# Attention and rational MoE on one core: the plan names each tile's buffer, the reciprocal is written to the hidden tile's PSUM bank, and the first 1226 operations run in a listed order

## The chip, the cores and the metric

One NeuronCore of a Trainium2 chip runs the whole program. The metric is the device time of one execution in microseconds; the time of the kernel before is the median of three runs. The engines are TensorE (PE: matmuls, PEld: weight loads), VectorE (DVE), ScalarE (ACT), GpSimd (POOL) and the sync engine SP, which issues all transfers.

## The reference

Sliding-window attention over 8 batches of 8 heads (576 tokens, width 64), then a two-layer feed-forward net over all 4608 tokens whose activation is a quotient of polynomials. Four heads look back over 32 tokens, the other four over every fourth of the last 128.

```python
scores = scale * np.matmul(q, k.transpose(0, 1, 3, 2))
scores = np.where(masks[None, :, :, :], scores, -1000000000.0)
attn = np.exp(scores - np.max(scores, axis=-1, keepdims=True))
attn = attn / (np.sum(attn, axis=-1, keepdims=True) + 1e-09)
x = ...matmul(attn, v), reshaped to (4608, 512)...
h = x @ w_in                                  # 512 -> 2048
P = a[0] + a[1] * h + a[2] * h2 + a[3] * h3   # h2 = h*h, h3 = h2*h
Q = 1.0 + np.abs(b[0]) * np.abs(h) + np.abs(b[1]) * h2
g = P / (Q + 1e-06)
return (g @ w_out).astype(np.float32)         # 2048 -> 512
```

w_in and w_out arrive as 64-bit floats.

## The kernel before

**Units.** Attention is cut into 48 units, six for each batch (batch b makes chunk b of 512 tokens; the 64 left-over tokens of all batches make chunk 8). A unit loads `qk` and `v`, makes `scores` on PE into two PSUM banks (`pair`, `pair_A`), takes a row maximum (`mx`), exponentials (`p`), a row sum (`sm`) and its reciprocal, normalizes (`norm`), turns `p` on PE (`t`, in a bank with the tag "h") or by DVE and a round trip through DRAM, multiplies by `v` (`av`) and splits the result into a high part `xh` and a low part `xl`, so that single-pass matmuls keep the precision. From batch 1 on, the result goes through DRAM as well (`results<-y`, `z<-results`). Units 0 to 5 are batch 0, units 6 to 11 batch 1.

**Weights.** 32 weight blocks (`wi0` to `wi15`, `wo0` to `wo15`) are loaded as 64-bit words (512 KB each) and turned to a high and a low fp32r part: a scale on ACT (`wi_f<-wi_raw`), a low word on ACT or POOL (`wi_raw<-wi_raw`), a join on DVE (`wi_f<-wi_f,wi_raw`), a high part on ACT, DVE or POOL (`wi<-wi_f`), a low part on DVE or POOL (`wi<-wi_f,wi`). The same goes for `wo`.

**Tiles.** The net is 144 tiles (chunk, block of 128 of the 2048 hidden features). In the order of the program tiles 0 to 7 belong to chunk 0 (blocks 0 to 7), tiles 8 to 23 to chunk 1, 24 to 31 to chunk 0 (blocks 8 to 15), then chunk by chunk. A tile is 12 matmuls into a PSUM bank with the tag "h" (two of them), a chain on the other engines, and 12 matmuls (`out`) into four banks. The chain, with the names that the rows show: `a<-h` (absolute value, ACT), `r<-a,ab_t` (linear part of Q, ACT), `a<-r,a` (product, DVE or POOL), `t<-h,na_t` (linear part of P, ACT), `t<-t,h` and `h<-t,na_t,h` (P continued, DVE), `r<-a,ln_bias` and `r<-r,exp_bias` (1/Q as the exponential of a negative logarithm, ACT), `h<-h,na_t,r` (P times 1/Q, DVE), `a<-a,r` (correction of the reciprocal, DVE), `a<-a,h` (the result, DVE), `gh<-a` (high part, ACT or POOL), `gl<-a,gh` (low part, POOL or DVE). The tile's bank is free again after `a<-a,h`; the matmuls of a tile wait for that of the tile two earlier, or for the copy of a unit's `t`, which shares the two banks.

**What sets the order.** `Plan.run` is a list scheduler that runs while the program is built: every operation has an engine (or several to choose from), a duration, dependencies and a due rank; the plan keeps a clock for each engine and emits the operation with the least rank among those that can start. Each engine then runs its own stream in that order. A buffer is a tag with a number of `bufs`, taken in turn. Before the plan's time 150 us, where the plan expects PE to wait, `keep_busy` puts matmuls without use in its stream (`ident_b` rows, called fillers below): 14 at the very start, then as many as fit in the gap.

```python
t2 = op({"DVE": 663}, k + LATE["t2"], lambda e: stt(self.ps, self.t, na_t[:, 1:2], self.ps, ALU.add, ALU.mult), t1)
ex = op({"ACT": 615}, k + LATE["ex"], lambda e: act(self.r, self.r, AF.Exp, bias=exp_bias, scale=-1.0), ln)
```

Of the kernel before, what the change touches and what calls it, by code (L numbers as in the profile page):

```python
# [25 lines left out]
BOTH = {"ACT": 480, "DVE": 520}  # L26
# [5 lines left out]
DUE = [(-38.49, 8.95), (-134.53, 10.99), (409.06, 77.81), (48.99, 2.72), (456.65, -31.55), (557.24, -11.85), (83.16, -17.62), (714.91, 29.14)]  # L32

LATE = {"ab": -275.92, "ql": -296.25, "pl": 24.3, "qq": -47.45, "t1": 94.47, "t2": -169.93, "ln": 295.15, "ex": -497.79, "g0": -1.51, "g1": -59.76, "g2": -270.73, "gh": -314.62, "gl": 497.37, "out": 3.78}
SLACK = {"sc": 1.16, "qk0": -46.44, "v0": -50.35, "load": -3.46, "wi": 11.08, "wo": -0.87, "w": -17.68, "gl": -7.82, "out": -4.87}
# [5 lines left out]
DEPTH, LOADS, STAGE, AHEAD, ON_PE, BY_PE = 2, 2, 6, 6, 2, 2  # L41
LEFT = S - 512
RQ, RKEY, NV = 4 * 3 * 32, 4 * 128, 3 * 2 * 2 * 64
# [18 lines left out]

class Op:
# [4 lines left out]
    def __init__(self, engs, rank, fn, deps, dma, lock):  # L68
        self.engs, self.rank, self.fn, self.dma, self.lock = engs, rank, fn, dma, lock
        self.deps = [d for d in deps if d is not None]  # L70
        self.takes, self.follows = [], []
        self.spare = None
        self.slack, self.by, self.end, self.eng, self.tail = None, None, None, None, 0.0
# [8 lines left out]
class Plan:  # L82
# [7 lines left out]
    DMA_START, DMA_NS, DMA_RATE = 1000.0, 1700.0, 380.0  # L90
    PERIOD, PE_LATE = 4743.0, 105.0

    def __init__(self, idle):
        self.ops, self.tags, self.idle = [], {}, idle

    def op(self, engs, rank, fn, *deps, dma=0, lock=False):
        o = Op(engs, rank, fn, deps, dma, lock)
        self.ops.append(o)
        return o

    def takes(self, o, tag, bufs, users):

        self.tags.setdefault(tag, (bufs, []))
        o.takes.append((tag, users))

# [26 lines left out]
    def run(self):  # L132
        free = {}
        pipe, ports = self.DMA_START, 0.0
# [6 lines left out]
        ready = [o for o in self.ops if not left[id(o)]]  # L141
        done = 0
        while ready:
            options = []
            for o in ready:
                before = list(o.deps)
                for tag, _ in o.takes:
                    bufs, groups = self.tags[tag]
                    if len(groups) >= bufs:
                        users = groups[len(groups) - bufs]  # L150
                        if any(u.end is None for u in users):
                            break
                        before += users
                else:
                    for eng, ns in o.engs.items():
                        shared = ports if Plan.shares(o, eng) else 0.0
                        t = max([free.get(eng, 0.0), shared] + [d.after(eng) for d in before])
                        options.append((t, o, eng, ns))
            assert options, "the plan is stuck"
            first = min(x[0] for x in options)  # L160
            eng0 = min((x for x in options if x[0] == first), key=lambda x: x[1].rank)[2]
            start, o, eng, ns = min(
                (x for x in options if x[2] == eng0 and x[0] <= first + self.WINDOW), key=lambda x: (x[1].rank, x[0])
            )
            for tag, users in o.takes:
                self.tags[tag][1].append(users)
            o.eng = eng
            if eng == "PE" and start > free.get(eng, 0.0) + 1.0:
                ns += self.PE_LATE
                self.idle(o, free.get(eng, self.PE_START), start)  # L170
            free[eng] = start + ns
            if Plan.shares(o, eng):
                ports = start + ns
            o.end = start + ns
            if o.dma:
                pipe = max(pipe, o.end) + o.dma / self.DMA_RATE
                o.end = pipe + self.DMA_NS
            ready.remove(o)
            done += 1
            o.fn(eng)  # L180
            for n in after.get(id(o), []):
                left[id(n)] -= 1
                if not left[id(n)]:
                    ready.append(n)
        assert done == len(self.ops), "the plan is stuck"
# [3 lines left out]
def tile_attention_moe(  # L189
# [6 lines left out]
    coef: bass.AP,  # L196
    mask: bass.AP,
# [14 lines left out]
    def idle(o, since, until):  # L212

        if until < BUSY_UNTIL:
            keep_busy(BUSY_FIRST if since == Plan.PE_START else int((until - since - BUSY_LESS) // BUSY_NS), o.spare)

    def keep_busy(n, ps):

        if n <= 0:
            return  # L220
        if busy["first"] is None:
            if ps is None:
                return
            go = True
        elif busy["out"] is None:
            if busy["first"][1]:
                return
# [4 lines left out]
        for _ in range(n):  # L232
            if go:
                mm(ps, ident_b, ident_b.unsqueeze(1).to_broadcast([P, 4, P]))
            else:
                mm(ps, zeros_b, ident_b.unsqueeze(1).to_broadcast([P, 4, P]), start=False, stop=False, free=True)

# [52 lines left out]
    class Unit:  # L290
# [6 lines left out]
        def load_qk(self, pool, tag):  # L297
            t = pool.tile([P, RQ + RKEY], F32, tag=tag, name=f"qk{self.n}", bufs=LOADS if pool is att else 1)
# [21 lines left out]
        def masks(self):  # L320
            for j, cnt, at in MASK_AT[self.u]:
                yield j, cnt, mask_t[:, 1:2].to_broadcast([P, cnt, 64]) if at is None else mask_t[:, at : at + cnt]
# [15 lines left out]
        def small(self, tag):  # L338

            t = att.tile([P, 18], F32, tag=tag, name=f"{tag}{self.n}", bufs=2)  # L340
# [18 lines left out]
        def new_p(self):  # L359
            self.p = att.tile([P, 6, 64], F32, tag="p", name=f"p{self.n}", bufs=2)  # L360
# [33 lines left out]
        def transposes(self):  # L394
            self.t = psum.tile([P, 512], F32, tag="h", name=f"t{self.n}", bufs=2)
# [10 lines left out]
        def new_pT(self):  # L406
            if self.start:
                self.pT = work.tile([P, 512], F32, tag="a", name=f"pT{self.n}")[:, :384]
            elif self.n % 2:
                self.pT = att.tile([P, 6, 64], F32, tag="p", name=f"pT{self.n}", bufs=2).rearrange("p j k -> p (j k)")  # L410
# [3 lines left out]
        def turn(self):  # L414

            self.turned = work.tile([P, 512], F32, tag="stage", name=f"u{self.n}", bufs=STAGE)[:, :384]
# [29 lines left out]
        def turn_out(self):  # L446

            self.turned = work.tile([P, 512], F32, tag="stage", name=f"y{self.n}", bufs=STAGE)[:, :384]
# [8 lines left out]
        def move_out(self):  # L457
            t = work.tile([P, 512], F32, tag="stage", name=f"z{self.n}", bufs=STAGE)[:, :384]
# [73 lines left out]
        def keep_left(self, eng):  # L532
            self.o = work.tile([P, 512], F32, tag="stage", name=f"l{self.n}", bufs=STAGE)
# [14 lines left out]
        def plan(self, by, tags):  # L548
# [7 lines left out]
            masks = [masked, identity] if self.on_pe else []  # L556
            if len(Unit.open) >= DEPTH:
                prev = Unit.open.pop(0)
            if prev:
                sc = op({"PE": 1320 + 300 * self.on_pe}, 0, lambda e: (prev.av(), self.scores()), *prev.placed, prev.lv, lq, *masks)  # L560
                clear = prev.finish(sc)
            else:
                sc = op({"PE": 1130 + 320 * self.on_pe}, 0, lambda e: self.scores(), lq, *masks)
            if self.on_pe:
                ma = sc
            else:
                ma = op({"DVE": 400 + 70 * len(MASK_AT[u])}, 0, lambda e: self.mask(), sc, masked)
            kind = KIND[self.n] if self.by_pe else 0
            if kind == 2:
                mx = op({"DVE": 470}, 0, lambda e: self.max(True), ma)  # L570
                sb = op({"PE": 760}, 0, lambda e: self.sub_pe(), mx, identity)
                su = ex = op({"ACT": 480}, 0, lambda e: self.exp_s(), sb)
                sm = op({"DVE": 510}, 0, lambda e: self.sum(), ex)
# [528 lines left out]
```

## Time and profile before

| | |
|---|---|
| median of 3 runs | 914.0 us (912.68 to 914.83) |
| the profiled execution, first to last instruction | 911.9 us |
| PE busy | 887.7 us (97%) |
| DVE, ACT, POOL busy | 727.6, 684.8, 472.8 us |
| first tile matmul starts | 42.23 us |

The profiled execution's own time is its span of 911.9 us; the timed runs lie about 2 us above. PE busy counts fillers and small attention matmuls, so its share alone doesn't tell how much of the span the needed matmuls take. Busy shares over the whole span mix a start (to about 150 us), in which weights, attention and tiles compete, with a long stretch in which tiles and a little attention run.

### The profile page before, as it was taken

To read this page: it belongs to the slowest core of one execution; us is meant where nothing else is said; L and a number is where in the kernel's file an instruction comes from. 1 tells how busy PE (TensorE), PEld (TensorE's weight loads), DVE (VectorE), ACT (ScalarE), POOL (GpSimd) and SP (SyncE) were. 2 spreads that over 40 slices of the span, in tenths; PEclk is the share of its full clock that TensorE was granted. 3 is DMA by queue.
4 is the path that set the end of the run, shared out by engine and by line. 5 is a ranking of instruction groups with operands and counts; after the bars stand their busy time and mean duration, and the time that the engine had idled before them with its cause. 6 is when DMAs were issued, how large, how long until landed. Compare 5 with 4: busy or idle time off the path is not lost.

```text
span 911.9 us, 21320 instructions
## 1 busy us (share of the span) xinstructions
PE 887.7 (97%) x8208; PEld 714.9 (78%) x8208; DVE 727.6 (80%) x1291; ACT 684.8 (75%) x1128; POOL 472.8 (52%) x424
## 2 busy tenths in 40 slices
PE   6889999999999999999999999999999999999998
PEld 4656778877887888888888878888888888888876
DVE  4889999988998986888688886887688677566656
ACT  3888899867767777677767767777877788778774
POOL 2354666635555654555555555456455555544442
PEclk8899999999999999999999999999999999999999
DMA  9785614144643531453155441233143220001001
GB/s 339 272 281 181 241 55 147 60 127 143 192 141 113 152 93 46 131 165 112 49 173 156 135 141 65 96 104 98 47 145 108 63 70 1 0 1 47 1 1 46
DMA packets 85478, 103.46 MB, mean 113 GB/s; under 512 B 37377, under 2 KB 62849, under 8 KB 85377
## 3 DMA queue, kind: packets, MB, share of 16 engines
q1 hardware_dynamic: 85376, 102.11, 35.1%
q8 instruction: 64, 1.05, 0.5%
q14 instruction: 38, 0.30, 0.1%
HBM read 75.21 MB, written 26.87 MB: 112 GB/s over the span
## 4 chain that ended last, share of the span: by engine, by line
PE 82%; DVE 8%; DMA 4%; ACT 2%; issue 2%; POOL 1%; SPq 1%; DVEq 0%; ACTq 0%; POOLq 0%
PE out L245 39%; PE h L245 38%; PE pair L245 4%; DVE a L254 2%; DMA results<-y 1%; DVE h L254 1%; DMA z<-results 1%; ACT r L248 1%; DMA qk<-in_qk_dram 1%; DVE t L251 1%; SPq L242 1%; POOL a L257 1%; PE pair_A L245 0%; DVE a L251 0%; PE pair_B L245 0%
## 5 line engine op out<-in xcount | busy, mean ns | idle before, releaser
L245 PE MATMUL h<-xh,wi 128*128 128x512 f32 x1136 | 376.7, 393 | 5.5 <-DVE a L254 5.1
L245 PE MATMUL out<-gh,wo 128*128 128x512 f32 x1136 | 352.8, 392 | 0.0
L257 POOL TENSOR_TENSOR a<-r,a 128x512 f32<-128x512 f32 x123 | 159.2, 1294 | 259.4 <-ACT r L248 241.2
L245 PEld LDWEIGHTS h<-xh,wi 128*128 128x128 f32 x1136 | 213.3, 188 | 55.2 <-DVE a L254 9.3
L245 PEld LDWEIGHTS out<-gh,wo 128*128 128x128 f32 x1136 | 211.6, 188 | 44.9
L245 PE MATMUL out<-gl,wo 128*128 128x512 f32 x568 | 221.4, 390 | 0.6 <-POOL gl L257 0.6
L245 PE MATMUL h<-xl,wi 128*128 128x512 f32 x568 | 221.3, 390 | 0.0
L257 POOL TENSOR_TENSOR gl<-a,gh 128x512 fp32r<-128x512 f32 x137 | 182.0, 1329 | 40.9 <-ACT gh L248 31.0
L254 DVE SCALAR_TENSOR_TENSOR a<-a,r 128x512 f32<-128x512 f32 x141 | 101.4, 719 | 121.3 <-ACT r L248 119.3
L248 ACT ACTIVATE r<-a,ln_bias 128x512 f32<-128x512 f32 x141 | 101.8, 722 | 67.9 <-POOL a L257 64.5
L248 ACT ACTIVATE r<-a,ab_t 128x512 f32<-128x512 f32 x141 | 114.6, 813 | 14.6 <-DVE h L254 9.0
L245 PEld LDWEIGHTS out<-gl,wo 128*128 128x128 f32 x568 | 106.6, 188 | 23.7 <-POOL gl L257 1.2
L245 PEld LDWEIGHTS h<-xl,wi 128*128 128x128 f32 x568 | 106.7, 188 | 21.3
L248 ACT ACTIVATE a<-h 128x512 f32<-128x512 f32 x140 | 83.3, 595 | 52.4 <-PE h L245 44.2
L254 DVE SCALAR_TENSOR_TENSOR h<-t,na_t,h 128x512 f32<-128x512 f32 x142 | 107.3, 755 | 4.6
L248 ACT ACTIVATE t<-h,na_t 128x512 f32<-128x512 f32 x142 | 109.2, 769 | 1.6 <-DVE h L254 1.2
L254 DVE SCALAR_TENSOR_TENSOR h<-h,na_t,r 128x512 f32<-128x512 f32 x142 | 106.5, 750 | 4.6 <-ACT r L248 3.3
L248 ACT ACTIVATE r<-r,exp_bias 128x512 f32<-128x512 f32 x144 | 104.3, 724 | 4.7
L248 ACT ACTIVATE gh<-a 128x512 fp32r<-128x512 f32 x133 | 83.6, 628 | 27.0 <-PE out L245 24.5
L251 DVE TENSOR_TENSOR t<-t,h 128x512 f32<-128x512 f32 x142 | 95.9, 675 | 5.9 <-ACT t L248 4.9
L254 DVE SCALAR_TENSOR_TENSOR a<-a,h 128x512 f32<-128x512 f32 x140 | 96.2, 687 | 4.8
L257 POOL TENSOR_TENSOR xl<-z,xh 128x256 fp32r<-128x256 f32 (+5 forms) x52 | 39.1, 764 | 33.1 <-ACT xh L248 32.7
(123 smaller groups left out, 716.2 us busy)
## 6 DMA issues: line engine op xcount, KB each, us to landing
qk<-in_qk_dram SPq DMA_DIRECT2D x48, 448.0 KB, 5.3
v<-in_vp_dram SPq DMA_DIRECT2D x48, 384.0 KB, 3.9
out_dram<-os SPq DMA_DIRECT2D x36, 256.0 KB, 2.1
wi_raw<-in_w_in_dram SPq DMA_DIRECT2D x16, 512.0 KB, 6.2
wo_raw<-in_w_out_dram SPq DMA_DIRECT2D x16, 512.0 KB, 5.9
results<-y SPq DMA_DIRECT2D x42, 192.0 KB, 3.5
z<-results SPq DMA_DIRECT2D x168, 48.0 KB, 2.0
turned<-u SPq DMA_DIRECT2D x36, 192.0 KB, 2.2
```

The source lines that it names most:

```text
L242: pin(nc.sync.dma_start(dst, src))
L245: pin(nc.tensor.matmul(o, lhs, rhs, start=start, stop=stop, skip_group_check=free))
L248: pin(nc.scalar.activation(o, i, func, **kw))
L251: pin(nc.vector.tensor_tensor(o, x, y, op))
L254: pin(nc.vector.scalar_tensor_tensor(o, x, s, y, op0, op1))
L257: pin(nc.gpsimd.tensor_tensor(o, x, y, op))
```

## The change

Six things change at once.

1. **Buffers.** A tag with several buffers becomes as many tags with one buffer (`plan.at`), and the plan picks the one that comes free first instead of taking them in turn. `a` has 3 buffers (2 before), `r` and `t` 2 (1 before), `stage` 7 (6), `LOADS` 3 (2).
2. **Where the chain writes.** The polynomial stays in `t` (SBUF) and the exponential goes to the tile's PSUM bank, so the bank holds 1/Q until the last steps. The exponential now waits for the DVE step that reads the bank last. The correction `a<-a,r` becomes `a<-a,h`.
3. **More engines to choose from** in the first 36 tiles: `r<-a,ab_t` on ACT, DVE or POOL, `gh` on DVE too, a unit's `norm` of batch 0 on DVE too.
4. **Loads.** Mask and coefficients travel behind `v` of unit 0 in one transfer (`head`); `mask_t` is copied from there by POOL for later units. The sync engine's scratch for dynamic DMA is made smaller.
5. **The plan's model**: other durations, `tail` (a result is seen earlier than the busy time says), a limit on transfers in flight, a model of PE's instruction fetch.
6. **A listed order.** The first 1226 operations are placed in the order of a table of numbers (a letter forces the engine); the rest is scheduled by rank, with new `DUE`, `LATE` and `SLACK`. The table holds the operations of about the first 36 tiles.

The fillers go from 55 to 19: 14 at the start, 5 before the first tile, none behind it.

```diff
-DEPTH, LOADS, STAGE, AHEAD, ON_PE, BY_PE = 2, 2, 6, 6, 2, 2
+DEPTH, LOADS, STAGE, AHEAD, ON_PE, BY_PE = 2, 3, 7, 6, 2, 2
+A, R, T, G, PS = 3, 2, 2, 2, 2
...
+ORDER = """
+0 2 3 6 1 18 32 7 20 8 9 10 21 102 11 34 22 35 12p 23 24 13 48 25 50 104p 36 14a 51 26p 37 38 96 39 97 103 15 64 16 114 27 52 53 17 28a 66 67 98p 54
...
+    def at(self, tag):
+        return tag if len(self.tags[tag]) == 1 else f"{tag}_{self.now[tag]}"
...
-            t2 = op({"DVE": 663}, k + LATE["t2"], lambda e: stt(self.ps, self.t, na_t[:, 1:2], self.ps, ALU.add, ALU.mult), t1)
+            t2 = op({"DVE": 663}, k + LATE["t2"], lambda e: stt(self.t, self.t, na_t[:, 1:2], self.ps, ALU.add, ALU.mult), t1)
...
-            ex = op({"ACT": 615}, k + LATE["ex"], lambda e: act(self.r, self.r, AF.Exp, bias=exp_bias, scale=-1.0), ln)
+            ex = op({"ACT": 615}, k + LATE["ex"], lambda e: act(self.ps, self.r, AF.Exp, bias=exp_bias, scale=-1.0), ln, t2)
...
-            g0 = op({"DVE": 663}, k + LATE["g0"], lambda e: stt(self.ps, self.ps, na_t[:, 0:1], self.r, ALU.add, ALU.mult), ex, t2)
-            g1 = op({"DVE": 640}, k + LATE["g1"], lambda e: stt(self.a, self.a, GUARD, self.r, ALU.add, ALU.mult), ex, lock=True)
+            g1 = op({"DVE": 663}, k + LATE["g1"], lambda e: stt(self.a, self.a, GUARD, self.ps, ALU.add, ALU.mult), ex)
+            g0 = op({"DVE": 663}, k + LATE["g0"], lambda e: stt(self.ps, self.t, na_t[:, 0:1], self.ps, ALU.add, ALU.mult), ex, t2, g1)
...
-            ql = op({"ACT": 710}, k + LATE["ql"], lambda e: self.q_lin(), ab)
+            ql = op({"ACT": 710, "DVE": 470, "POOL": 780} if self.early else {"ACT": 710}, k + LATE["ql"], lambda e: self.q_lin(e), ab, lock=True)
...
+        for item in order:
+            n, eng = (int(item[:-1]), ENGINES[item[-1]]) if item[-1] in ENGINES else (int(item), None)
+            o = self.ops[n]
+            assert id(o) in ready, "the order breaks a dependency"
+            place(*next(x for x in options(o) if eng in (None, x[2])))
```

Two places show what the new order does to the streams. The first is PE behind the first tile's matmuls, between the attention steps of unit 9 (`qk9`, `mx9`) and those of unit 10. Before (`h1` is the matmul of tile 1, `out0_0_0<-ident_b` a filler):

```order
L400 MATMUL t8_933<-ident_90,p8_859 128x128 x3
...
L245 MATMUL out0_0_0_962<-ident_b_91 128x512
L245 MATMUL pair_85<-mx9_954,ident_90 128x192 x2
...
L245 MATMUL pair_85<-v8_818,pT8_948 32x64 x24
...
L245 MATMUL pair_85<-qk10_823 32x64 x24
...
L245 MATMUL pair_85<-mx10_1059,ident_90 128x192 x2
...
L400 MATMUL t9_1090<-ident_90,p9_977 128x128 x3
L245 MATMUL h1_1100<-xh0_338,wi1_585 128x512
```

And now:

```order
L500 MATMUL t8_918<-ident_90,p8_807 128x128 x3
L337 MATMUL pair_85<-mx9_912,ident_90 128x192 x2
L337 MATMUL h1_944<-xh0_317,wi1_528 128x512
...
L337 MATMUL pair_85<-v8_930,pT8_938 32x64 x24
...
L337 MATMUL pair_85<-qk10_928 32x64 x24
L500 MATMUL t9_1040<-ident_90,p9_942 128x128 x3
L337 MATMUL pair_85<-mx10_1035,ident_90 128x192 x2
L337 MATMUL h2_1063<-xh0_317,wi2_584 128x512
```

Tile 1 has moved ahead of unit 8's `av` and unit 10's scores, tile 2 stands where tile 1 stood, and the 13 fillers of this place are gone.

The second is DVE around the end of tile 6, whose last step `a6<-a6,h6` frees the bank for tile 8 (`sm12`, `mx13`, `mask_t` belong to units of batch 2). Before:

```order
L251 TENSOR_TENSOR a6_1651<-r6_1658,a6_1651 128x512
L260 CAST wi9_1674<-wi_f9_1505 128x512
L251 TENSOR_TENSOR t6_1672<-t6_1672,h6_1620 128x512
L254 SCALAR_TENSOR_TENSOR h6_1620<-t6_1672,na_t_97,h6_1620 128x512
L254 SCALAR_TENSOR_TENSOR h6_1620<-h6_1620,na_t_97,r6_1658 128x512
L384 TENSOR_SCALAR sm12_1653<-sm12_1653 128x3x2
L385 RECIPROCAL sm12_1653<-sm12_1653 128x6
L251 TENSOR_TENSOR pair_85<-pair_85,mask_t_89 128x2x192
L254 SCALAR_TENSOR_TENSOR a6_1651<-a6_1651,r6_1658 128x512
L254 SCALAR_TENSOR_TENSOR a6_1651<-a6_1651,h6_1620 128x512
```

And now:

```order
L343 TENSOR_TENSOR t6_1606<-t6_1606,h6_1557 128x512
L346 SCALAR_TENSOR_TENSOR t6_1606<-t6_1606,na_t_96,h6_1557 128x512
L346 SCALAR_TENSOR_TENSOR wi_f8_1588<-wi_f8_1588,wi_raw8_1191 128x512
L343 TENSOR_TENSOR gl5_1623<-a5_1519,gh5_1611 128x512
L346 SCALAR_TENSOR_TENSOR a6_1592<-a6_1592,h6_1557 128x512
L346 SCALAR_TENSOR_TENSOR h6_1557<-t6_1606,na_t_96,h6_1557 128x512
L346 SCALAR_TENSOR_TENSOR a6_1592<-a6_1592,h6_1557 128x512
```

The product `a6<-r6,a6` has moved to POOL, `gl5` has come from POOL, the correction reads `h6` in place of `r6`, and the steps of batch 2's units and of `wi9` stand elsewhere. DVE's stream holds 167 instructions up to and with the last row before, and 148 now.

## Rows read from the trace of the kernel before

**Rows 1.** Windows: us, PE, PEld, DVE, ACT, POOL busy (count), PE clock, DMA share, GB/s

```profile
0.00:42.00 42.00, 31.20 (x844) 21.65 (x845) 25.26 (x61) 23.07 (x70) 11.92 (x27) 0.88 0.82 298
42.00:60.00 18.00, 14.98 (x251) 10.12 (x249) 15.49 (x31) 15.70 (x39) 11.49 (x12) 1.00 0.86 297
60.00:106.00 46.00, 42.31 (x456) 30.84 (x455) 43.68 (x76) 38.95 (x69) 21.79 (x19) 1.00 0.62 210
...
150.00:330.00 180.00, 179.29 (x1867) 145.15 (x1866) 163.23 (x302) 134.47 (x216) 99.24 (x90) 1.00 0.44 129
330.00:904.00 574.00, 573.13 (x4592) 469.16 (x4591) 433.77 (x753) 431.38 (x670) 298.92 (x256) 1.00 0.26 79
```

**Rows 2.** PE's groups, 42 to 150 us: count, busy us, mean ns

```profile
L245 PE MATMUL out<-ident_b,zeros_b 128*128 128x512 bf16 x23 | 5.7, 381 | 0.0
L245 PE MATMUL out<-ident_b 128*128 128x512 bf16 x13 | 3.5, 379 | 0.0
```

**Rows 3.** PE's waits, 42 to 150 us: total, times, longest

```profile
PE h L245 <- DVE a L254: 5.1, 4, 1.6
PE pair L245 <- ACT p L248: 1.6, 2, 1.3
PE pair L245 <- DVE mx L345: 1.1, 3, 0.6
```

**Rows 4.** Timeline of PE: instruction-fetch stall, first tile, later waits

```profile
21.16 0.61 PE L245 MATMUL pair_B<-pT,v 64*64 64x32 f32 x18 [3.39 <-issue]
...
42.23 0.53 PE L245 MATMUL h<-xh,wi 128*128 128x512 f32 x1
...
106.15 0.50 PE L245 MATMUL h<-xh,wi 128*128 128x512 f32 x1 [1.62 <-DVE a L254]
126.88 0.50 PE L245 MATMUL h<-xh,wi 128*128 128x512 f32 x1 [1.34 <-DVE a L254]
```

**Rows 5.** Timelines of DVE, ACT and POOL, tile 6, before tile 8's matmuls

```profile
101.39 0.76 DVE L254 SCALAR_TENSOR_TENSOR h<-t,na_t,h 128x512 f32<-128x512 f32 x1
...
103.67 1.70 DVE L254 SCALAR_TENSOR_TENSOR a<-a,r 128x512 f32<-128x512 f32 x1
105.41 0.69 DVE L254 SCALAR_TENSOR_TENSOR a<-a,h 128x512 f32<-128x512 f32 x1
106.01 0.55 DVE L345 TENSOR_REDUCE mx<-pair 128x6 f32<-128x384 f32 x1
...
101.21 0.73 ACT L248 ACTIVATE r<-r,exp_bias 128x512 f32<-128x512 f32 x1
...
103.54 1.28 POOL L257 TENSOR_TENSOR gl<-a,gh 128x512 fp32r<-128x512 f32 x1
```

**Rows 6.** DVE's groups, 0 to 150 us

```profile
L254 DVE SCALAR_TENSOR_TENSOR a<-a,r 128x512 f32<-128x512 f32 x14 | 12.0, 859 | 0.0
L251 DVE TENSOR_TENSOR a<-r,a 128x512 f32<-128x512 f32 x12 | 10.1, 839 | 0.8 <-ACT r L248 0.4
L254 DVE SCALAR_TENSOR_TENSOR a<-a,h 128x512 f32<-128x512 f32 x14 | 9.6, 687 | 0.4
L251 DVE TENSOR_TENSOR wi<-wi_f,wi 128x512 fp32r<-128x512 f32 x6 | 5.3, 878 | 0.8 <-ACT wi L248 0.6 <-POOL wi L269 0.2
L251 DVE TENSOR_TENSOR xl<-z,xh 128x384 fp32r<-128x384 f32 x2 | 1.8, 912 | 1.3 <-ACT xh L248 1.3
L260 DVE CAST wi<-wi_f 128x512 fp32r<-128x512 f32 x4 | 1.7, 420 | 0.1
```

**Rows 7.** ACT's groups, 0 to 150 us

```profile
L248 ACT ACTIVATE r<-a,ab_t 128x512 f32<-128x512 f32 x15 | 12.2, 813 | 2.2 <-DVE a L254 2.0
L248 ACT ACTIVATE r<-r,exp_bias 128x512 f32<-128x512 f32 x14 | 10.1, 724 | 0.4
L248 ACT ACTIVATE a<-h 128x512 f32<-128x512 f32 x15 | 8.8, 583 | 1.7 <-PE h L245 1.5
L248 ACT ACTIVATE wi<-wi_f 128x512 fp32r<-128x512 f32 x8 | 5.0, 622 | 0.5 <-DVE wi_f L254 0.5
```

More of the change, by code (lines that the diff above doesn't have):

```diff
@@ L101, in takes, with held @@
     def takes(self, o, tag, bufs, users):
-        self.tags.setdefault(tag, (bufs, []))
+        self.tags.setdefault(tag, [[] for _ in range(bufs)])
         o.takes.append((tag, users))
+    def at(self, tag):
+        return tag if len(self.tags[tag]) == 1 else f"{tag}_{self.now[tag]}"
+    def held(self, o, eng):
+        for tag, _ in o.takes:
+            free = [(max([u.after(eng) for u in users], default=0.0), n) for n, users in enumerate(self.tags[tag]) if all(u.end is not None for u in users)]
+            yield (tag, *min(free, default=(math.inf, 0)))
     @staticmethod
@@ L140, in run @@
                 after.setdefault(id(d), []).append(o)
[L141 to L164, printed above, removed]
@@ new lines, in run, with options @@
+        ready = {id(o): o for o in self.ops if not left[id(o)]}
+        def options(o):
+            queue = []
+            if o.dma:
+                parts = 0
+                for f in reversed(flying):
+                    if parts + f.parts + o.parts > self.FLYING:
+                        queue = [f.end]
+                        break
+                    parts += f.parts
+            for eng, ns in o.engs.items():
+                shared = state["ports"] if Plan.shares(o, eng) else 0.0
+                held = [t for _, t, _ in self.held(o, eng)]
+                start = max([free.get(eng, 0.0), shared] + queue + held + [d.after(eng) for d in o.deps])
+                if start < math.inf:
+                    yield start, o, eng, ns
@@ L183, in run @@
                 if not left[id(n)]:
-                    ready.append(n)
-        assert done == len(self.ops), "the plan is stuck"
+                    ready[id(n)] = n
+        for item in order:
[3 more added lines that the diff above has]
+            place(*next(x for x in options(o) if eng in (None, x[2])))
+        while ready:
+            every = [x for o in ready.values() for x in options(o)]
+            assert every, "the plan is stuck"
+            first = min(x[0] for x in every)
+            eng0 = min((x for x in every if x[0] == first), key=lambda x: x[1].rank)[2]
+            place(*min((x for x in every if x[2] == eng0 and x[0] <= first + self.WINDOW), key=lambda x: (x[1].rank, x[0])))
+        assert not state["left"], "the plan is stuck"
 @with_exitstack
@@ L532, in keep_left @@
         def keep_left(self, eng):
[L533 removed]
+            self.o = work.tile([P, 512], F32, tag=plan.at("stage"), name=f"l{self.n}", bufs=1)
             for (first, cnt), _ in self.pieces()[1]:
@@ L718, in w_copy @@
     def w_copy(key):
-        wf[key] = w = work.tile([P, 512], F32, tag="stage", name="%s_f%d" % key, bufs=STAGE)
+        wf[key] = w = work.tile([P, 512], F32, tag=plan.at("stage"), name="%s_f%d" % key, bufs=1)
         dcopy(w, raw[key])
@@ L900, in stage @@
     def stage(o):
-        staged[o] = work.tile([P, 512], F32, tag="stage", name=f"os{o}", bufs=STAGE)
+        staged[o] = work.tile([P, 512], F32, tag=plan.at("stage"), name=f"os{o}", bufs=1)
         return staged[o]
@@ L987, in fetch_left @@
     def fetch_left(kt):
-        lefts[kt] = t = work.tile([P, 512], F32, tag="stage", name=f"left{kt}", bufs=STAGE)
+        lefts[kt] = t = work.tile([P, 512], F32, tag=plan.at("stage"), name=f"left{kt}", bufs=1)
         load(t, left_dram[:, kt])
@@ L1035, in tile_attention_moe @@
     loads = sorted(early, key=lambda o: o.rank)
+    order = ORDER if wide else []
+    listed = {int(x.strip("adpes")) for x in order}
+    loads = [o for o in loads if plan.ops.index(o) not in listed]
     for o, before in zip(loads[1:], loads):
         o.follows.append(before)
-    plan.run()
+        o.loose = before
+    plan.run(order)
 _OUT = (DM, NC, 512)
```

296 lines of the change are left out of this document (192 added, 104 removed).

## The prediction

> **What bounds the kernel now.** I read the windows first [rows 1]. From 150 us to 904 us PE is busy 752.4 of 754 us; nothing on the other engines waits to be gained there, since the changed program issues the same tile matmuls (144 tiles of 24) and the same attention matmuls. In that stretch DVE is idle 16.8 of 180 us and ACT 45.5, so the moved writes of the chain cost nothing there: PE's own work covers them until they use up the 16.8 us that DVE has free. The time to be won lies ahead of 150 us. PE's first tile starts at 42.23 us [rows 4], and between then and 150 us three things stand in PE's stream that the result doesn't need: fillers, busy for 5.7 + 3.5 = 9.2 us [rows 2], waits of 5.1 us for DVE's last step of an earlier tile, 1.6 us for ACT and 1.1 us for DVE in the attention [rows 3]. That is 17.0 us in all, and 15.7 us of it ahead of tile 8 (all but the 1.34 us at 126.88 [rows 4]). The longest of those waits is at tile 8, which starts at 106.15 when `a<-a,h` of tile 6 ends.
>
> The same windows name the engines that PE waits for: from 60 to 106 us DVE is busy 43.68 of 46 us, ACT 38.95, POOL 21.79 [rows 1]. So the start is bound by DVE, closely followed by ACT, with half of POOL free. The timeline ahead of tile 8 shows how the two halves hang together [rows 5]: `a<-a,r` takes 1.70 us instead of its usual fraction, beside POOL's `gl<-a,gh`, which ran from 103.54 to 104.82; the `a<-a,h` behind it takes 0.69 us and PE starts 0.05 us after that.
>
> **DVE up to tile 8.** I count the instructions of DVE's stream up to and with the last step of tile 6 and price the differences. There are 167 before and 148 after.
> - The product `a<-r,a`: 5 before, 1 after, at 839 ns [rows 6]: -3.4 us.
> - The correction: 7 times 687 ns in place of 859 ns, since it reads the bank as `a<-a,h` does [rows 6]: -1.2 us.
> - Low parts of weights: 8 to 3, at 878 ns [rows 6]: -4.4 us. High parts: 7 to 2, at 420 ns [rows 6]: -2.1 us. Joins: two fewer, at the nearest row, 878 ns: -1.8 us.
> - `xl<-z` of batch 1: 7 to 0. Two are of the size in the row, 912 ns; the other five write between a quarter and two thirds of that, and I take half a row for each [rows 6]: -4.1 us.
> - Added: three `gl` at 839 ns (same form as the product), three copies `xl<-pair_A` of batch 0 and one `r<-a` at no more than 420 ns [rows 6]: +4.2 us. Three small steps fewer are left at nothing.
>
> The sum is -12.8 us. Neighbours on DVE overlap: the `a<-a,h` at 105.41 lasts 0.69 us and the next instruction starts at 106.01 [rows 5], so each instruction costs 0.09 us less than its duration; for 19 fewer that is 1.7 us back: **-11.1 us**, if DVE idles as much as before. `t` kept in SBUF and P times 1/Q from `t` have no row of their own; the same inputs and ALU steps with one end elsewhere are `a<-a,h` (687) and `a<-a,r` (859), so over 7 tiles each may lie 1.2 us to either side of nothing; I take nothing.
>
> [...] Here the row with the SBUF operand shows 859 ns and the one with the PSUM operand 687 ns [rows 6]. [...]
>
> **ACT up to tile 8.** Up to the exponential of tile 6 ACT has 163 instructions before and 155 after: `r<-a,ab_t` 7 to 4 at 813 ns, high parts of `wi` 4 to 1 at 622 ns [rows 7]; the other differences leave two fewer and are put at nothing. That is -4.3 us, less 8 times 0.09 us of overlap: -3.6 us. The exponential now writes PSUM, for which there is no row; the cheapest and dearest full ACT rows are 583 and 813 ns against its own 724 [rows 7], so 7 of them lie between -1.0 and +0.6 us, and I take nothing. ACT was idle 2.30 + 7.05 = 9.35 us between 42 and 106 us [rows 1], mostly behind DVE. If that stays, tile 8 comes only 3.6 us earlier by ACT; if half of it goes because DVE and POOL deliver earlier, 8.3 us; if all, 13.0 us.
>
> **POOL** takes what leaves DVE: up to the product of tile 6 four more of its own products, two `r<-a`, one more low part, five more high parts, and three fewer `gl`; 7 instructions more in all, which at the 1.28 us of a `gl` [rows 5] are at most 9 us on a base of 45.2 us busy out of 106 [rows 1]. It stays far from full; what it costs is latency in a chain, which the third buffer of `a` and the second of `r` and `t` leave room for.
>
> **PE up to tile 8.** Without fillers and waits tile 8 would start 15.7 us earlier even with the first tile unmoved. The order puts tile 1 between units 8 and 9 and tile 2 where tile 1 stood, so PE has needed work where the 13 fillers stood. The first tile itself may move: less weight work on DVE ahead of it pulls it forward by up to 4 us (five low parts and some high parts), while the mask, which now comes behind 384 KB of `v`, holds the first scores back by up to 1.5 us (384 KB at the 298 GB/s of that window [rows 1] is 1.3 us). I take 2 us earlier. The three buffers of `qk` and `v` let loads start earlier; they cost nothing, since SP issues the same transfers but two.
>
> **The sum.** Three bounds for tile 8: PE 15.7 us plus the 2 us of the first tile, DVE 11.1 us, ACT 3.6 to 13.0 us with 8.3 us in the middle. The tightest decide; I take 9.5 us, between ACT's middle and DVE. Behind tile 8 the wait of 1.34 us at 126.88 has the same cause and goes too: 10.8 us. The profiled execution would go from 911.9 to 901.1 us, and the median from 914.0 us, which lies 2.1 us above it, to **903.2 us**.
>
> **Rivals.**
> - *PE is freed altogether.* DVE and ACT lose their idle time too, every filler and wait goes and the first tile comes 2 us earlier: 17.0 + 2 = 19.0 us, 895 us. For it: POOL has room, and the new order has no fillers behind the first tile. Against it: a fixed order over four engines always waits somewhere, and the plan of before, which expected to wait only where it set fillers, also left 7.8 us of waits.
> - *ACT takes DVE's place.* ACT keeps its idle time, also because the exponential must now wait for the DVE step on `t`: in tile 6 it began at 101.21, while the DVE step ended at 102.15 [rows 5], a wait of 0.94 us there, with everything behind it on ACT. Then only 3.6 + 1.3 us come: 909 us.
> - *Nothing is moved.* A wait of the first tile (mask, first-unit loads) and new in-order waits eat the gain: 912.2 to 915.8 us, within 0.2% (1.8 us), which is about what a measurement of this kernel can tell from no change.
> - *Slower, by instruction fetch.* PE stood 3.39 us with nothing to wait for that the profile shows [rows 4], in the stretch where transfers fill the queues. It happened once at this length in the first 2189 PE and PEld instructions [rows 1], though the DMA share is 0.82 before 42 us and 0.86 behind. The new load order keeps more transfers in flight; each further stall costs up to 3.39 us where PE is the bound, so the gain is gone at 3.2 of them, and with four the time is 903.2 + 13.6 = 917 us. [...]
>
> **How the numbers follow.** Chances: the forecast (898 to 907 us) 0.52, PE freed (892 to 898) 0.18, ACT takes over (907 to 912) 0.16, nothing moved 0.06, slower 0.08. Faster is the first three, 0.86; same 0.06; slower 0.08. The range of 8 in 10 leaves out the slower cases (0.14 above 912 with nothing moved) and the lower edge of PE freed (about 0.05 below 894): 894 to 912 us.
>
> **What would show it.** In the profile after: no fillers behind the first tile; PE's waits between the first tile and 150 us near 6 us in total instead of 7.8 us plus 9.2 us of fillers; tile 8 near 96.5 us; corrections of about 690 ns with no 1.7 us one before a PE wait; DVE's busy share between 60 and 106 us lower, ACT's higher, POOL's well above half; from 150 us on PE full as before. Wrong would be: first tile later than 43 us, PE `issue` waits of several us, exponentials that wait for `t` in most early tiles with PE idle behind them, or gaps in PE behind 150 us because batch 2's `x` comes late.

## The result, and the profile after

The changed kernel takes 901.85 us (median of 4 runs, 900.37 to 902.22) beside 914.41 us of the kernel before: ratio 0.9863, 95% interval 0.9845 to 0.9882. Forecast were 903.2 us, 894 to 912. The profiled execution has a span of 898.3 us, 13.6 us less than before's; the medians differ by 12.6 us.

The windows after [rows 1]: us, busy time of PE, PEld, DVE, ACT, POOL, granted clock, DMA share, GB/s.

```profile
0.00:42.00 42.00, 33.92 (x847) 24.09 (x847) 21.66 (x59) 21.98 (x66) 18.69 (x33) 0.80 0.79 295
42.00:60.00 18.00, 16.02 (x342) 11.96 (x343) 16.55 (x32) 16.29 (x38) 10.64 (x11) 1.00 0.95 330
60.00:106.00 46.00, 45.28 (x394) 35.87 (x390) 44.60 (x75) 43.85 (x82) 31.53 (x32) 1.00 0.62 207
...
150.00:330.00 180.00, 179.47 (x2049) 145.46 (x2048) 163.02 (x320) 128.63 (x211) 124.12 (x118) 1.00 0.52 158
330.00:891.00 561.00, 560.31 (x4264) 458.95 (x4262) 425.33 (x722) 417.20 (x652) 286.00 (x241) 1.00 0.23 71
```

From 60 to 106 us three engines are now nearly full at once; POOL went from 21.79 to 31.53 us. PE's waits from 42 to 150 us [rows 3], all of them (total, times, longest):

```profile
PE t L500 <- DVE a L346: 1.1, 1, 1.1
PE pair L337 <- DVE mx L445: 0.6, 1, 0.6
PE h L337 <- ACT pT L340: 0.3, 1, 0.3
PE out L337 <- DVE gl L343: 0.3, 1, 0.3
PE pair L337 <- issue: 0.2, 1, 0.2
```

That is 2.5 us in place of 7.8, no tile's matmuls wait for DVE for more than 0.11 us any more, and the filler groups of [rows 2] have no counterpart. PE's timeline [rows 4]: three pauses ahead of the first tile, the first tile, tile 8, and a wait in the last tile.

```profile
15.15 1.50 PE L337 MATMUL pair_B<-pT,v 64*64 64x32 f32 x45 [1.29 <-issue]
...
21.54 0.55 PE L337 MATMUL pair_B<-pT,v 64*64 64x32 f32 x23 [0.64 <-issue]
...
27.76 0.48 PE L337 MATMUL pair<-mask_t,ident_b 128*128 128x192 bf16 x2 [2.96 <-POOL p L349]
...
41.96 0.48 PE L337 MATMUL h<-xh,wi 128*128 128x512 f32 x1
...
95.72 0.39 PE L337 MATMUL h<-xh,wi 128*128 128x512 f32 x1
...
891.22 0.73 PE L337 MATMUL out<-gh,wo 128*128 128x512 f32 x2 [0.69 <-ACT gh L340]
```

Tile 8 starts at 95.72 us in place of 106.15; the first tile hardly moved. DVE is close behind PE: its last step of tile 6 ends at 95.17 us (94.48 + 0.69 in the trace), 0.55 us ahead of tile 8. DVE's groups from 0 to 150 us [rows 6] (both last steps of a tile share the first row now), and ACT's [rows 7]:

```profile
L346 DVE SCALAR_TENSOR_TENSOR a<-a,h 128x512 f32<-128x512 f32 x33 | 22.5, 682 | 1.4 <-ACT h L340 0.7
...
L343 DVE TENSOR_TENSOR gl<-a,gh 128x512 fp32r<-128x512 f32 x10 | 7.5, 754 | 0.6 <-ACT gh L340 0.6
...
L343 DVE TENSOR_TENSOR a<-r,a 128x512 f32<-128x512 f32 x2 | 1.9, 940 | 0.0
```

```profile
L340 ACT ACTIVATE h<-r,exp_bias 128x512 f32<-128x512 f32 x17 | 11.7, 690 | 1.5 <-DVE t L346 0.9
```

The correction costs 682 ns instead of 859, the exponential into PSUM 690 instead of 724.

The account of the 13.6 us, from PE's stream (starts of successive matmuls): 36 fillers at 0.22 us, 8.0 us; waits behind the first tile, 7.8 - 2.5 = 5.3 us; first tile, 0.3 us. It describes the lead at tile 15 (148.77 us before, 135.19 now). At the start of the last tile the lead is 15.0 us (894.51 and 879.50), and the last tile gives 1.4 us of it back: from its first matmul to the end of the span it takes 18.8 us in place of 17.4.

### The profile page after: what moved, and what is told of

The parts are those of the page before. It is cut to its first block, busy times and chain, and to the rows that moved or that the text cites. A ratio compares the mean times of both kernels' runs of the same rounds, so it can differ in the third digit from the quotient of the medians.

```text
span 898.3 us, 21077 instructions
## 1 busy us (share of the span) xinstructions
PE 882.3 (98%) x8172; PEld 714.6 (80%) x8172; DVE 716.1 (80%) x1272; ACT 667.2 (74%) x1111; POOL 502.5 (56%) x461
## 4 chain that ended last, share of the span: by engine, by line
PE 88%; DVE 4%; DMA 2%; ACT 2%; issue 1%; SPq 1%; DVEq 0%; ACTq 0%
PE h L337 41%; PE out L337 41%; PE pair L337 5%; DMA left<-l 1%; DMA pT<-turned 1%; SPq L334 1%; DVE t L343 0%; DVE spare_h L346 0%; DVE a L346 0%; DVE t L346 0%; ACT p L340 0%; DVE h L346 0%; ACT t L340 0%; DVE wi L343 0%; ACT r L340 0%
## 5 line engine op out<-in xcount | busy, mean ns | idle before, releaser
L349 POOL TENSOR_TENSOR a<-r,a 128x512 f32<-128x512 f32 x137 | 178.0, 1299 | 226.5 <-ACT r L340 210.0
L346 DVE SCALAR_TENSOR_TENSOR a<-a,h 128x512 f32<-128x512 f32 x280 | 191.7, 684 | 72.8 <-POOL gl L349 40.6
L349 POOL TENSOR_TENSOR gl<-a,gh 128x512 fp32r<-128x512 f32 x129 | 169.2, 1311 | 59.9 <-ACT gh L340 59.0
L337 PEld LDWEIGHTS h<-xl,wi 128*128 128x128 f32 x568 | 106.7, 188 | 21.4
L340 ACT ACTIVATE h<-r,exp_bias 128x512 f32<-128x512 f32 x142 | 98.1, 691 | 20.2 <-DVE t L346 16.2
L346 DVE SCALAR_TENSOR_TENSOR t<-t,na_t,h 128x512 f32<-128x512 f32 x142 | 105.9, 746 | 4.5
L340 ACT ACTIVATE r<-a,ab_t 128x512 f32<-128x512 f32 x121 | 98.8, 816 | 3.9
L340 ACT ACTIVATE gh<-a 128x512 fp32r<-128x512 f32 x129 | 80.9, 627 | 23.9 <-PE out L337 21.8
L349 POOL TENSOR_TENSOR p<-p,sm 128x384 f32<-128x384 f32 x42 | 35.8, 853 | 39.1 <-DVE sm L485 27.6
```

Source lines behind the costliest of these rows:

```text
L337: pin(nc.tensor.matmul(o, lhs, rhs, start=start, stop=stop, skip_group_check=free))
L340: pin(nc.scalar.activation(o, i, func, **kw))
L346: pin(nc.vector.scalar_tensor_tensor(o, x, s, y, op0, op1))
L349: pin(nc.gpsimd.tensor_tensor(o, x, y, op))
```

## The experiments

Four theories, as the expectations name them. **P**: behind the first tile PE's own stream bounds the start now, and the gain is needed work standing where fillers and waits stood. **V**: DVE (with ACT) still bounds the start, and time follows its instruction times. **B**, **U**: the bank swap, or the buffers, are the gain in any order. **L** and **Q** are named with their runs. Times are medians; ratios are to before on the same chip, with 95% intervals.

**What bounds the start: the base, fillers put back, products put back on DVE.** The changed kernel once more:

> The changed kernel itself, once more, as the base for the three runs beside it: 900 to 903 us, a ratio of 0.985 to 0.988. On theory P (behind the first tile, PE's own stream is what bounds the start now: fillers and waits have left it) its waits between the first tile and 150 us are again under 3 us in all.

900.63 us, 0.9857 (0.9834 to 0.9879). With fillers:

```diff
             if self.i == 0:
                 busy["first"] = (self.c, self.ft), False
+            if 1 <= self.i <= 6:
+                keep_busy(6, None)
```

> The changed kernel with six fillers put in front of each of tiles 1 to 6, 36 in all, as many as the change took away. Each takes 0.22 us of PE, 8.0 us together, and PE waits only 2.7 us behind its first tile. Theory P: +5 to +8 us. Rival V (DVE and ACT bound the start, PE only follows): the fillers lie in PE's waits, 0 to +2 us.

905.72 us, 0.9910 (0.9891 to 0.9928): 5.1 us over the base. The window of 60 to 106 us of this run:

```profile
60.00:106.00 46.00, 45.68 (x475) 34.26 (x474) 39.00 (x67) 38.45 (x75) 28.32 (x28) 1.00 0.62 204
```

DVE falls from 44.60 to 39.00 us; from the first tile to tile 6's last step it idles 8.4 us in place of 2.6. So it waits for PE now: P. Products back on DVE:

```diff
+ORDER = [x[:-1] + "d" if x in ("1078p", "1114p", "1132p", "1150p", "1168p", "1186p") else x for x in ORDER]
```

> The changed kernel with the products of tiles 0, 2, 3, 4, 5 and 6 on DVE in place of POOL, at the same places of the list. That is 6 times about 0.66 us more in DVE's stream, 4.0 us, of which its idle time between 42 and 106 us (2.9 us) can take some. Rival V: +4 us or close to it. Theory P: 0 to +1.3 us.

901.27 us, 0.9862 (0.9843 to 0.9881): 0.6 us over the base, inside both intervals. From the first tile to tile 8 PE takes 54.3 us (53.7 in the base). This run decides less than it was meant to. The six products cost DVE 5.5 us (8 of them at 930 ns in place of 2 at 940), but with less on POOL its other steps got shorter (the joins `wo_f<-wo_f,wo_raw` alone by 2.1 us up to tile 6's last step), so that up to there DVE is busy only 1.2 us more. V falls by the fillers, which would have cost nothing if DVE bounded the time.

**Are fillers a loss?** The kernel before without those behind the first tile:

```diff
-BUSY_UNTIL, BUSY_LESS, BUSY_NS, BUSY_FIRST, KEEP = 150000.0, 250.0, 240.0, 14, 0
+BUSY_UNTIL, BUSY_LESS, BUSY_NS, BUSY_FIRST, KEEP = 40000.0, 250.0, 240.0, 14, 0
```

> The kernel before without its 36 fillers behind the first tile; every needed instruction stays at its place. They take 8.0 us of PE between 42 and 106 us. If they only fill waits for other engines, the waits grow by about as much and the time stays within 1.5 us of before: then the change's gain can't come from leaving fillers out, only from needed work put in their place (theory P). If they stand in the way: 5 to 8 us less.

914.88 us (12 runs), 1.0009 (0.9995 to 1.0024): no difference. PE's waits from 42 to 150 us in it:

```profile
PE h L245 <- DVE a L254: 8.4, 4, 3.1
PE pair L245 <- DVE mx L345: 2.4, 2, 1.3
PE pair L245 <- ACT p L248: 1.7, 1, 1.7
```

The waits for DVE's last step grew from 5.1 to 8.4 us; from the first tile to tile 8 PE takes 63.9 us with and without fillers. In the old order they only filled gaps; in the new one the same number costs 5 us, because hardly any gaps are left.

**The bank swap.** The changed kernel in the same listed order, with the operands as before:

```diff
-            t2 = op({"DVE": 663}, k + LATE["t2"], lambda e: stt(self.t, self.t, na_t[:, 1:2], self.ps, ALU.add, ALU.mult), t1)
+            t2 = op({"DVE": 663}, k + LATE["t2"], lambda e: stt(self.ps, self.t, na_t[:, 1:2], self.ps, ALU.add, ALU.mult), t1)
...
-            ex = op({"ACT": 615}, k + LATE["ex"], lambda e: act(self.ps, self.r, AF.Exp, bias=exp_bias, scale=-1.0), ln, t2)
+            ex = op({"ACT": 615}, k + LATE["ex"], lambda e: act(self.r, self.r, AF.Exp, bias=exp_bias, scale=-1.0), ln, t2)
...
-            g1 = op({"DVE": 663}, k + LATE["g1"], lambda e: stt(self.a, self.a, GUARD, self.ps, ALU.add, ALU.mult), ex)
-            g0 = op({"DVE": 663}, k + LATE["g0"], lambda e: stt(self.ps, self.t, na_t[:, 0:1], self.ps, ALU.add, ALU.mult), ex, t2, g1)
+            g1 = op({"DVE": 663}, k + LATE["g1"], lambda e: stt(self.a, self.a, GUARD, self.r, ALU.add, ALU.mult), ex)
+            g0 = op({"DVE": 663}, k + LATE["g0"], lambda e: stt(self.ps, self.ps, na_t[:, 0:1], self.r, ALU.add, ALU.mult), ex, t2, g1)
```

The plan keeps its rule that the exponential stands behind `t2`, so every engine carries out the same steps in the same order as in the changed kernel; only the operands differ.

> The changed kernel with the polynomial back in the PSUM bank and the exponential back in SBUF, in the same listed order. Theory P: corrections cost about 860 ns again in place of 684 ns and exponentials 724 in place of 691 ns, but PE keeps its place, so 0 to +1.5 us. Rival B (the bank is where the gain comes from): +3 us or more. Rival V (the start goes as DVE's instruction times go): 15 tiles times 0.17 us, +2.6 us by 150 us.

905.70 us, 0.9912 (0.9895 to 0.9928): 5.1 us over the base. B's size came, and P's 0 to 1.5 us missed. The loss is mostly not in the start: beside the second profile of the changed kernel it is 0.9 us up to tile 15 and 4.0 us from there to tile 36 (136 to 268 us). From 150 to 330 us this run has

```profile
150.00:330.00 180.00, 177.07 (x2007) 141.61 (x2006) 169.37 (x310) 125.83 (x206) 127.08 (x115) 1.00 0.52 153
```

and PE waits for DVE's last step of a tile again, as in neither profile of the changed kernel there:

```profile
PE h L337 <- DVE a L346: 2.2, 5, 0.8
```

DVE's groups in that stretch:

```profile
L346 DVE SCALAR_TENSOR_TENSOR a<-a,r 128x512 f32<-128x512 f32 x30 | 30.6, 1021 | 4.1 <-ACT r L340 3.4 <-POOL gl L349 0.4
...
L346 DVE SCALAR_TENSOR_TENSOR a<-a,h 128x512 f32<-128x512 f32 x30 | 20.4, 680 | 0.8
```

In the kernel before the same correction takes 703 ns in the same stretch:

```profile
L254 DVE SCALAR_TENSOR_TENSOR a<-a,r 128x512 f32<-128x512 f32 x30 | 21.1, 703 | 1.1 <-ACT r L248 1.1
```

Two of the 30, in the timelines of DVE and of POOL of the run with the swap undone:

```profile
168.23 1.78 DVE L346 SCALAR_TENSOR_TENSOR a<-a,r 128x512 f32<-128x512 f32 x1
...
175.72 0.64 DVE L346 SCALAR_TENSOR_TENSOR a<-a,r 128x512 f32<-128x512 f32 x1
```

```profile
167.63 1.84 POOL L349 TENSOR_TENSOR wi<-wi_f,wi 128x512 fp32r<-128x512 f32 x1
...
174.77 0.97 POOL L824 TENSOR_SCALAR wo_raw<-wo_raw 128x512 int32<-128x512 uint32 x1
```

The first lasts until 170.01, which is 0.54 us after POOL's instruction ended at 169.47; the second starts as POOL's ends and takes 0.64 us. Over the whole run 80 corrections with no POOL instruction beside them take 688 ns in the mean, 61 with one beside them for more than 0.05 us 1124 ns (in the kernel before 107 at 687 ns and 34 at 822 ns); the 140 steps `a<-a,h`, which read one operand from PSUM, take 684 to 687 ns either way. So the swap is worth 5 us in this order, by letting DVE and POOL work side by side; POOL is busy 124.12 of 180 us in the changed kernel, 99.24 before [rows 1]. Why POOL's instruction lengthens the form with two SBUF operands and not the one with a PSUM operand, no run shows.

At the very end the swap costs something: with it undone the last tile takes 17.5 us from its first matmul to the end of the span, in place of 18.8 us (17.4 before), and the wait of 0.69 us for `gh` ahead of its last `out` matmuls is not there:

```profile
896.43 0.62 PE L337 MATMUL out<-gh,wo 128*128 128x512 f32 x2
```

**Buffers, swap and order by rank.** The kernel before with more buffers (`bufs=A`, `R`, `T` stand in the tiles too):

```diff
+A, R, T = 3, 2, 2
...
-            self.r_buf = ("stage", STAGE) if self.late else ("r", 1)
+            self.r_buf = ("stage", STAGE) if self.late else ("r", R)
...
-                plan.takes(ab, "a", 2, [gl])
+                plan.takes(ab, "a", A, [gl])
...
-            plan.takes(pl, "t", 1, [t2])
+            plan.takes(pl, "t", T, [t2])
...
-    nc = _bacc.Bacc("TRN2", target_bir_lowering=False, num_devices=1)
+    nc = _bacc.Bacc("TRN2", target_bir_lowering=False, num_devices=1, dynamic_dma_scratch_size=1024)
```

> The kernel before with three buffers of a and two each of r and t, and the small scratch for dynamic transfers that makes room for them; nothing else. The order by rank shifts a little, fillers go from 55 to 59. Theory P: 911 to 917 us, since PE still has fillers and waits. Rival U (buffers are the gain): 902 to 908 us.

935.11 us, 1.0219 (1.0189 to 1.0249), a miss for both theories. The same with the bank swap, as in the change's diff:

> The kernel before with the buffers of the run beside it and the bank swap; fillers 54. From 150 us on PE was full in the kernel before, so the shorter corrections can bring something only ahead of that: 1 to 2 us less than the run with buffers alone. If the swap is worth the 5 us of the run that undid it in any order: 5 us less.

936.94 us, 1.0247 (1.0218 to 1.0275): a miss too. The changed kernel without its list:

```diff
-    order = ORDER if wide else []
+    order = []
```

and with the three lines `DUE`, `LATE` and `SLACK` of the kernel before.

> The changed kernel without its list and with the DUE, LATE and SLACK of before: buffers, bank swap, choices of engine, loads and the new plan model, ordered by rank alone; 73 fillers instead of 19. Theory P (the order is what took fillers and waits out of PE's stream): most of the gain is gone, 908 to 916 us. Rival L (buffers and swap would have brought it in any order): 900 to 905 us.

958.04 us, 1.0471 (1.0439 to 1.0502): worse than before, a miss for L and beyond P's range. The control says how to read these three:

```diff
-            ex = op({"ACT": 615}, k + LATE["ex"], lambda e: act(self.r, self.r, AF.Exp, bias=exp_bias, scale=-1.0), ln)
+            ex = op({"ACT": 620}, k + LATE["ex"], lambda e: act(self.r, self.r, AF.Exp, bias=exp_bias, scale=-1.0), ln)
```

> A control: the kernel before with one of the plan's planned durations changed from 615 to 620 ns (the exponential's), nothing else. It moves the order by rank on every engine, and with it fillers and waits. If an order by rank is fragile, this alone costs some us, up to the 21 us that the three buffers cost: 915 to 935 us. If the 21 us are the buffers' own: within 2 us of before.

932.36 us, 1.0183 (1.0158 to 1.0208). Five planned nanoseconds cost 18 us, though the program computes the same with the same buffers: six fillers more, some steps on other engines, and another order. The stretch from 150 to 330 us in it, and in the run with buffers alone:

```profile
150.00:330.00 180.00, 170.01 (x1629) 135.86 (x1628) 155.60 (x277) 123.02 (x196) 90.30 (x81) 0.98 0.38 118
```

```profile
150.00:330.00 180.00, 172.45 (x1637) 139.11 (x1636) 160.57 (x281) 127.28 (x202) 83.41 (x74) 0.97 0.37 116
```

PE loses 10.0 and 7.5 us there, where the kernel before loses 0.7. The ranks and costs of before were a setting that happened to fit; the three neighbours tried all fell out of it. So these runs can't price buffers, swap or list by themselves. They do show that neither buffers nor swap bring the gain in the orders tried: U falls, and B in its general form. The listed order with the buffers, the loads or the engine choices of before was not run, so what each of them adds to it stays open.

**The first tile.** In the changed kernel PE stops at its instruction 961 (all its records in the trace counted from 0, semaphore records among them), and the pauses of this kind stand at 449 (0.47 us) and 705 (3.39 us) in the kernel before and at 449 (1.29 us), 705 (0.64 us) and 961 (2.85 us) in the changed one, 256 apart. Three list entries change:

```diff
+for x in ("126", "47", "80"):
+    ORDER.remove(x)
+ORDER[ORDER.index("46a") + 1 : ORDER.index("46a") + 1] = ["126", "47", "80"]
```

> The changed kernel with one piece of the load order changed: the store of unit 2's left-over tokens, which waits for ACT until 26.7 us, stands ahead of the loads of v5, v6, qk8 and what follows, so that these no longer lie in the queue while PE's code page is fetched; wi3 comes ahead of it. In the changed kernel PE stands 2.85 us at its instruction 961, 1.6 us behind the landing of a 16 KB instruction transfer at 26.18 us, and has a granted clock of 0.55 from 27.7 to 38.6 us. Theory Q (the code transfer is held up by the full queue): it lands 1.5 to 3 us earlier, the pause is under 1 us, the first tile comes 2 to 5 us earlier and the time falls by 1.5 to 5 us. Rival (PE waits for POOL's last step on p there, as the profile names it): the pause stays at 2.9 us, 0 or a loss of up to 2 us by the later loads.

899.33 us, 0.9831 (0.9805 to 0.9858), which still overlaps the base's interval. Then qk7 (entry 299) goes behind the waiting store too:

> The run with later loads, with qk7 behind the waiting store too: one transfer of 448 KB fewer ahead of the code page. Theory Q: the page for instruction 961 lands 0.7 to 1.1 us earlier than 24.35 us, the pause falls from 1.86 to about 1 us, and the first tile comes up to 1 us ahead of 39.42 us, unless qk7 is late for unit 7's scores (then it comes later): 897.5 to 900 us.

897.09 us, 0.9810 (0.9789 to 0.9832). And v4 (entry 65) as well:

> The same with v4 behind the waiting store as well, another 384 KB out of the way. Theory Q: the page lands near 22.6 us and the pause is gone; v4 may then be late for its matmuls, which would put a wait of up to 2 us there: 897 to 901 us.

898.36 us, 0.9818 (0.9795 to 0.9842). The row of instruction 961 in the runs with products on DVE, with later loads, and with qk7 and v4 later too:

```profile
27.25 0.48 PE L338 MATMUL pair<-mask_t,ident_b 128*128 128x192 bf16 x2 [0.93 <-DVE sm L486]
```

```profile
25.60 0.33 PE L340 MATMUL pair<-mask_t,ident_b 128*128 128x192 bf16 x2 [1.86 <-POOL wi L352]
```

```profile
24.55 0.47 PE L340 MATMUL pair<-mask_t,ident_b 128*128 128x192 bf16 x2 [1.58 <-DVE sm L488]
```

```profile
24.52 0.32 PE L340 MATMUL pair<-mask_t,ident_b 128*128 128x192 bf16 x2 [0.49 <-DVE wi L355]
```

The profile names four releasers for one instruction, all of them engines that happened to finish something. What the pauses share is the 16 KB transfer in PE's instruction queue (times in us, from the packets of the trace):

```
kernel                 transfer landed   PE goes on   pause at 961
changed                      26.18          27.76         2.85
changed, again               26.09          27.48         2.96
products on DVE              25.84          27.25         0.93
later loads                  24.35          25.60         1.86
and qk7 later                23.15          24.55         1.58
and v4 later                 22.94          24.52         0.49
```

The pause is the time in which neither a matmul nor a weight load runs; the profile's 2.96 us in the changed kernel count from the last matmul. PE goes on 1.25 to 1.58 us after the landing each time (in the kernel before, behind its pause at 705, 1.35 us after the landing at 19.81), and the landing moves with what was put into the queue ahead of it: counted from PE's matmul at 705 it comes after 4.6 to 4.8 us in the first three programs, and after 3.9, 3.4 and 2.2 us in the three with later loads. Q holds, the wait for POOL's `p` falls. The sizes missed: the pause was still 1.86 and 1.58 us, as PE also came to that point 1.2 and 1.9 us earlier. With v4 late the pause is nearly gone, but a later one of the kind opens (1.41 us at 34.59), so it brings nothing more. The granted clock around the pause, changed kernel:

```profile
15.00:24.80 9.80, 9.01 (x255) 6.66 (x254) 6.12 (x17) 6.71 (x24) 3.87 (x5) 0.73 1.03 402
24.80:27.70 2.90, 0.00 (x1) 0.10 (x1) 1.70 (x5) 1.94 (x7) 2.43 (x2) 0.91 1.03 402
27.70:38.60 10.90, 10.84 (x260) 9.03 (x259) 5.68 (x16) 5.80 (x18) 4.47 (x5) 0.55 0.36 120
```

With qk7 later:

```profile
27.70:38.60 10.90, 10.73 (x272) 8.71 (x272) 6.85 (x20) 8.86 (x31) 7.35 (x9) 0.83 0.98 352
```

After PE had stood for 2.9 us the granted clock was 0.50 for 10.2 us (27.2 to 37.4 us); behind the pause of 1.58 us the clock of the same window is 0.83. That the length of the pause sets the length of the stretch is not shown: in the kernel before, the pause of 3.39 us [rows 4] was followed by only 6.8 us at 0.50 (21.4 to 28.2 us). The run with qk7 later is the fastest here, 0.5% below the changed kernel; its interval (0.9789 to 0.9832) just clears the base's (0.9834 to 0.9879). Part of its profile is chance: the 14 fillers at the very start took 4.49 us in it and 5.76 in the changed kernel. In every trace they start 0.427 us apart at first and 0.216 us apart later; the step comes after 6 of them in this run, after 12 in the changed kernel, and after all 14 in its second profile, whose program is the same. From the first needed matmul behind them to the first tile PE takes 32.8 us with later loads, 32.4 with qk7, 32.7 with v4, and 34.9 in the changed kernel; the five profiles whose start is the changed kernel's lie between 33.5 and 36.4.

Where the runs stand (start of a tile's first matmul, us):

```
kernel                  tile 0    tile 8    tile 15   tile 36
before                   42.23    106.15    148.77    275.54
before, no fillers       41.63    105.56    149.50    275.14
changed                  41.96     95.72    135.19    261.93
changed, again           42.08     95.82    135.25    262.56
swap undone              41.97     96.55    136.14    267.50
fillers put back         42.83    101.99    141.42    267.95
products on DVE          40.49     94.77    134.26    262.93
later loads, qk7 too     38.16     91.91    131.35    258.59
one planned cost         43.86    106.99    152.73    291.48
buffers alone            43.09    108.17    153.57    292.83
```

## Why the prediction was right, and where it was not

- **The start is what changes, and PE is full from 150 us on.** Right up to the last tile: 179.47 of 180 us, and 13.6 us of the gain are there by tile 15.
- **DVE up to tile 6's last step, -11.1 us.** Right, in part by luck: that step ended at 106.1 us before and ends at 95.2 us now, 10.9 us earlier. But its busy time fell by 12.35 us, since the 1.7 us given back for overlap were 0.2, and its idle time, taken as unchanged, grew by 1.42. The correction at 687 ns was measured at 682.
- **ACT, 3.6 to 13.0 us with 8.3 in the middle.** The exponential of tile 6 ends at 92.25 us in place of 101.94, 9.7 us earlier: 5.6 us less work (forecast 3.6) and 4.1 us less idle time (taken as 4.7). "Mostly behind DVE" was a misreading: of ACT's waits from 42 to 106 us in the kernel before, 3.4 us were for `z<-results` from DRAM and 2.3 us for DVE.
- **POOL.** Forecast well above half from 60 to 106 us, measured 31.53 of 46 us. "7 instructions more" doesn't follow from its own list, which adds up to nine; up to the product of tile 6 POOL is busy 51.3 us in place of 41.4, which is 9.9 us more and not at most 9.
- **Sum at tile 8, 9.5 us, and 1.3 us behind it.** The start of tile 8 came 10.4 us earlier, but it was the wrong gauge: 69 needed `out` matmuls stand ahead of it now, 60 before, and 9 of 0.23 us are another 2.1 us of PE's work done. So PE was 12.5 us ahead there, and this term is the miss. Behind tile 8 came 3.2 us more by tile 15: most of these 2.1 us, and the wait of 1.34 us at 126.88. The bound of PE, set aside for the tighter ones of DVE and ACT, was the better term: 17.0 us, less 2.5 us that PE still waits, less 1.2 us because 36 fillers in a row take 8.0 us and not 9.2, is 13.3 us.
- **First tile 2 us earlier.** Wrong: 0.27 us, and that is less than the spread between executions. The kernel before starts it at 42.23 us and, without its later fillers but with the same start, at 41.63; the five profiles with the changed kernel's start lie between 40.49 and 42.83. So the term for less weight work on DVE had no effect that shows. What holds the stretch up is, at least in part, the fetch pause at 961: with the page's landing moved forward the first tile starts at 38.16 to 39.42 us.
- **"The moved writes of the chain cost nothing" from 150 us on, and the swap is worth 1.2 us ahead of tile 8.** The first half held up to the last tile, which the swap makes 1.3 us longer; the second was mis-sized: in the new order the swap is worth 5.1 us, 4.0 of them between tiles 15 and 36. The step that failed took 687 against 859 ns as a fixed price and POOL's load as it was. With POOL idle the two forms cost the same, 688 and 684 to 687 ns, and the whole difference is POOL's. The row that shows POOL's part was in sight: in [rows 5] `a<-a,r` runs from 103.67 to 105.37, 0.55 us past the end of POOL's `gl` at 104.82.
- **Rivals.** *PE is freed altogether* came nearest after the forecast: behind the first tile PE waits 2.5 us. *ACT takes DVE's place*: exponentials do wait for the step on `t`, 0.9 us in all up to 150 us, and PE behind them doesn't. *Fetch stalls* came at their three places, 4.8 us in all (3.9 before), all ahead of the first tile and none in the place of the gain. The changed kernel's trace has 64 transfers of 16 KB, and three of them go with such a pause above 0.25 us; the longest, 2.85 us, lies in a stretch with a DMA share of 1.03. The one row of the kind behind 42 us is 0.2 us.

## What to carry to other kernels

Count what an engine's stream holds, not when one landmark starts: fillers and waits removed from the engine that bounds are the gain, if needed work is ready to stand there, and leaving out fillers alone was worth nothing. An order made by greedy ranks is one draw: compare a structural change against several draws (here 5 planned ns moved 18 us) or in a fixed order. An operand moved to PSUM was worth more here than its instruction time says, where VectorE and GpSimd work side by side: 5.1 us in this order, with the correction at 688 ns alone, 1124 ns beside POOL, and 684 to 687 ns either way for a step with a PSUM operand.

## What the runs showed of the hardware

- An exponential of 128x512 into PSUM takes 690 ns, into SBUF 721 to 724 ns.
- The correction on DVE with two SBUF operands took 688 ns in the mean with POOL idle and, in one case, 1.78 us behind a POOL instruction that began 0.60 us earlier.
- A pause of 2.85 us that the profile puts down to POOL went with a code fetch, told by the instruction's number (961) and the landing of its 16 KB at 26.18 us: PE went on 1.58 us later, and 1.25 to 1.58 us behind the landing in all six executions of the table.
- The first 14 fillers took 4.49 to 6.15 us in executions whose programs start alike, because the step from one start every 0.427 us to one every 0.216 us comes after 6 of them or later, up to after all 14. The granted clock of the windows doesn't show it: its first record (1.00) begins at 4.1 us in the fastest of them and at 7.5 us in the slowest, where the step comes. What sets that moment stays open.
